# One Strassen pair in the first FFN of blocks 3 to 6, and queries of batches 4 to 7 scaled at their cast

## The chip, the cores and the metric

The kernel runs on 1 core of a Trainium2 chip. The metric is the device time in microseconds (us). It is the span of the trace, from the first to the last instruction, and about 2.2 us more outside of it. The engines are TensorE (PE in the profile; PEld is its weight load), VectorE (DVE), ScalarE (ACT), GpSimd (POOL), and SyncE (SP), which issues the transfers. All runs that are compared here are fast runs with a granted TensorE clock of 0.99 to 1.00. In the profile's lines, L810 is line 810 of that run's kernel. The same statement has another number in each of the two kernels: settle's addition is L810 before and L828 after the change, and scan's addition and multiplication are L522 and L526 before, L533 and L537 after.

## The reference

A retention layer (attention with a decay mask in place of the softmax) feeds a feed-forward network (FFN) with a GELU:

```python
# q, k, v: (8, 8, 576, 64) float32: batch, heads, sequence, head width
scores = (q @ k.transpose(0, 1, 3, 2)) / sqrt(64)
gamma  = 1.0 - 2.0 ** (-5.0 - arange(8))                # one per head
Dmat   = where(i >= j, gamma_h ** (i - j), 0.0)
attn   = (scores * Dmat) @ v
x = attn.transpose(0, 2, 1, 3).reshape(4608, 512)
h = x @ w_in                                            # (4608, 512) @ (512, 2048)
g = 0.5 * h * (1 + tanh(sqrt(2 / pi) * (h + 0.044715 * h**3)))
out = g @ w_out                                         # (4608, 2048) @ (2048, 512)
```

## The kernel before

The work is cut into nine blocks of 512 tokens: Block(b) holds the first 512 tokens of batch b, and Block(None) the last 64 of all eight batches (the "tails"). They run in the order 0, 1, ..., 6, None, 7. Attention runs in chunks, one batch ahead of the FFN: `score_mm` (TensorE) and `mask_sc` (VectorE), `state_mm` (TensorE), `scan` (VectorE) and `put` (a cast of the running state), then `values` and `inter_mm` (TensorE) and `evac` (VectorE).

The first FFN of a block is sixteen columns `up`, each four matmuls of 512 columns and a gelu. The second FFN is one level of Strassen in seven products, my, mz, mw, mv, mu, my2, mz2. The `mix_*` helpers prepare its inputs and `settle` adds its products up. In the last two blocks, four pairs of first-FFN columns are computed by one Strassen level too: `pair_a`, `pair_q`, `pair_b`, `pair_s`, `pair_g`. A pair needs sums and differences of the weights (`forms_w`, ten quarter-tiles for each pair) and of the inputs (`forms_x`, five for each block).

```python
def bank(name, dt=F32):               # all matmul outputs share eight PSUM banks
    return ps.tile([128, 512 if dt == F32 else 1024], dt, tag="bank", name=name)

def score_mm(b, s, hh):
    st = [bank("st") for _ in range(2)]
    ...                               # 16 small matmuls

def scan(b, n, hhs=(0, 1)):           # reads the banks of state_mm
    ...
    if n > 0:
        nc.vector.tensor_tensor(out=t, in0=uc, in1=a["w", n - 1][:, qs], op=ALU.add)        # vs
    nc.vector.tensor_tensor(out=a["w", n][:, qs], in0=uc, in1=gt..., op=ALU.mult)           # ws

def evac(b, s, c):
    nc.vector.tensor_tensor(out=xb[b]..., in0=att[b]["x", s][c]..., in1=gx, op=ALU.mult)

class Block:
    def up(self, f):
        hp = bank("hp")
        for ct in range(4):
            nc.tensor.matmul(hp, w_in_sb[:, ct, 128 * f : 128 * f + 128], x[:, :, ct, :], ...)
        nc.scalar.activation(out=self.g(f // 2)[:, f % 2], in_=hp, func=AF.Gelu_apprx_tanh)

    def pair_a(self, j):              # 10 matmuls of 256 columns into three banks
        pv, pw, py = bank("pv"), bank("pw"), bank("py")
        ...
    def pair_q(self, j):              # one ScalarE copy, two VectorE operations
        ...
    def pair_b(self, j):              # 4 more matmuls onto py
        ...
    def settle(self, m, u=None):      # reads the bank of product m
        ...
        if m == "my":   nc.scalar.mul(out=q(0, 1), in_=t, mul=-1.0)
        ...
        elif m == "mv":
            tt(q(0, 0), q(1, 1), ALU.subtract)      # tt: nc.vector.tensor_tensor
            tt(q(0, 1), q(0, 1), ALU.add)
        ...
    def down(self, m):
        self.product(m)
        self.settle(m)
```

In the timelines below each engine works through its instructions in program order, and the program order is a schedule by hand. `units` are the pieces of TensorE's FFN work; `plan` says after which unit a side step is emitted.

```python
def run(units, plan):
    for i, f in enumerate(units):
        f()
        for step in plan.get(i, ()):
            step()
...
units += [L(F2.up, f) for f in range(NF)] + [L(F2.down, m) for m in MS]   # units 56 to 71, 72 to 78
plan = add({},
    ...
    (73, L(mask_tail, 3)),
    (76, L(scan, 4, 0)),
    (77, L(scan, 4, 2)),
    (78, L(put, 4, 0, S2)),           # S2: half on ScalarE, half on VectorE
    (76, L(scan, 4, 1)),
    ...
)
run(units, plan)
...
for t in order:                       # blocks 3 to 6, None, 7: the same plan for each of 3 to 6
    ...
    plan = add({},
        (1, L(values_tail, t)),
        (1, L(score_mm, b, 0, 1)),    # b = t + 1
        (1, L(score_mm, b, 0, 0)),
        (1, L(inter_tail, t)),
        ...
```

## Time and profile before

| before | |
|---|---|
| device time, median (lowest to highest) | 297.97 us (297.75 to 298.04) |
| span of the profiled execution | 295.8 us |
| busy share of the span: TensorE, VectorE, ScalarE, GpSimd | 98%, 80%, 55%, 33% |
| granted TensorE clock | full in every slice |

The busy shares are averages over stages with different limits, and the end of a matmul is estimated, so the table says which engine is full but not where the time goes.

### The profile page before, as it was taken

Reading aid. Unit: us, or ns where it says so; the run is one execution under the profiler, and the core shown is the slowest. Engines: PE = TensorE matmul, PEld = TensorE weight load, DVE = VectorE, ACT = ScalarE, POOL = GpSimd, SP = SyncE. Lnnn points to the kernel's source line nnn. Section 1 sums busy time; section 2 is a strip of 40 time slices with the busy share of each in tenths; the row PEclk is TensorE's granted clock in tenths of the full one; section 3 lists DMA queues with packets and bytes.
Section 4 is the critical chain, followed back from the end, with each engine's and each line's share of the span. In section 5 each row is a group of like instructions: output and inputs, shape, how many; then the busy total and the mean of one; then the engine's idle time right before and its main releaser. Section 6 shows DMA issues by size and latency. Waiting matters only on the chain.

```text
span 295.8 us, 8812 instructions
## 1 busy us (share of the span) xinstructions
PE 289.7 (98%) x3689; PEld 207.1 (70%) x3689; DVE 237.2 (80%) x456; ACT 164.1 (55%) x320; POOL 99.0 (33%) x131
## 2 busy tenths in 40 slices
PE   8999999999999999999999999999999999999995
PEld 5657478888885568656875587558755886787684
DVE  4898889989997999888569856899688198876773
ACT  7449889973736681665446544554445317605830
POOL 4662695056160346075037007698000000000000
PEclk9999999999999999999999999999999999999999
DMA  7999999767899979995996999482120002002204
GB/s 224 336 350 313 307 381 316 201 173 189 219 227 228 298 224 162 286 308 110 215 303 193 161 240 264 121 155 9 58 86 2 1 33 112 2 0 73 71 0 144
DMA packets 92663, 52.48 MB, mean 177 GB/s; under 512 B 38352, under 2 KB 86480, under 8 KB 92624
## 3 DMA queue, kind: packets, MB, share of 16 engines
q1 hardware_dynamic: 92288, 51.26, 65.2%
q10 hardware_dynamic: 336, 0.66, 0.8%
q8 instruction: 29, 0.48, 0.7%
q14 instruction: 10, 0.08, 0.1%
HBM read 36.70 MB, written 9.44 MB: 156 GB/s over the span
## 4 chain that ended last, share of the span: by engine, by line
PE 85%; ACT 4%; DVE 3%; POOL 2%; DMA 2%; SPq 1%; issue 1%; DVEq 0%; POOLq 0%
PE hp L641 29%; PE my L783 10%; PE mz L783 9%; PE hp L727 6%; PE mu L783 5%; PE mv L783 5%; PE mw L783 5%; PE xs L553 3%; PE py L671 2%; PE xs L580 2%; DMA ld<-in_v_dram 2%; PE st L438 2%; POOL cv L260 1%; SPq L197 1%; PE pv L671 1%; PE us L506 1%
## 5 line engine op out<-in xcount | busy, mean ns | idle before, releaser
L641 PE MATMUL hp<-x,w_in_sb 128*128 128x512 f16 x400 | 92.4, 379 | 0.4 <-DVE vs L522 0.2
L645 ACT ACTIVATE gT<-hp 128x512 f16<-128x512 f32 x108 | 63.9, 597 | 43.9 <-PE hp L641 43.1
L641 PEld LDWEIGHTS <-w_in_sb 128*128 128x128 f16 x432 | 40.9, 98 | 42.9 <-issue 0.6
L783 PEld LDWEIGHTS <-gT 128*128 128x128 f16 x576 | 55.8, 98 | 8.1 <-ACT gT L714 0.2
L451 DVE TENSOR_TENSOR ret<-st,cm 128x512 f16<-128x512 f32 x64 | 40.0, 681 | 4.5 <-PE st L438 4.5
L260 POOL TENSOR_TENSOR cv<-ld,sc 128x512 f16<-128x512 f32 x28 | 30.8, 1115 | 33.2 <-DMA ld<-in_v_dram 33.2
L247 POOL CAST kq<-ld 128x512 f16<-128x512 f32 x27 | 18.8, 704 | 56.8 <-DMA ld<-in_k_dram 33.5
L247 ACT CAST tbd<-ws 64x256 f16<-64x256 f32 x56 | 22.3, 402 | 22.3 <-DVE ws L526 21.8
L783 PE MATMUL my<-w_out_sb,gT 128*128 128x256 f16 x288 | 34.5, 273 | 0.0
L783 PE MATMUL mz<-w_out_sb,gT 128*128 128x256 f16 x288 | 34.4, 273 | 0.0
L783 PEld LDWEIGHTS <-gsum 128*128 128x128 f16 x288 | 27.9, 98 | 3.4
L756 DVE TENSOR_TENSOR gT<-gT 128x1024 f16<-128x1024 f16 x35 | 28.8, 842 | 0.2
L752 DVE TENSOR_TENSOR gsum<-gT 128x1024 f16<-128x1024 f16 x35 | 27.8, 795 | 1.3 <-ACT gT L733 0.8
L593 DVE TENSOR_TENSOR x<-xs,gx 128x512 f16<-128x512 f32 x32 | 21.7, 684 | 4.0 <-PE xs L580 3.6
L810 DVE TENSOR_TENSOR ost<-ost,mv 128x512 f32<-128x512 f32 x18 | 11.6, 683 | 11.7 <-issue 7.7
L744 DVE TENSOR_TENSOR gdia<-gT 128x512 f16<-128x512 f16 (+1 forms) x32 | 16.3, 508 | 5.0 <-ACT gT L645 2.6
L727 PE MATMUL hp<-x,w_in_sb 128*128 128x256 f16 x160 | 18.8, 273 | 0.0
L247 ACT CAST kq<-ld 128x512 f16<-128x512 f32 x27 | 16.4, 616 | 4.0 <-DMA ld<-in_q_dram 2.8
L783 PE MATMUL mw<-w_out_sb,gdia 128*128 128x256 f16 x144 | 17.2, 273 | 0.0
L783 PE MATMUL mu<-w_out_sb,gsum 128*128 128x256 f16 x144 | 17.2, 273 | 0.0
L783 PE MATMUL mv<-w_out_sb,gsum 128*128 128x256 f16 x144 | 17.2, 273 | 0.0
L727 PEld LDWEIGHTS <-w_in_sb 128*128 128x128 f16 x160 | 15.3, 98 | 2.2 <-issue 0.3
(119 smaller groups left out, 396.2 us busy)
## 6 DMA issues: line engine op xcount, KB each, us to landing
ld<-in_k_dram SPq DMA_DIRECT2D x30, 256.0 KB, 5.1
ld<-in_q_dram SPq DMA_DIRECT2D x30, 256.0 KB, 5.1
ld<-in_v_dram SPq DMA_DIRECT2D x30, 256.0 KB, 5.5
out_dram<-ost SPq DMA_DIRECT2D x14, 512.0 KB, 4.3
loan<-in_moe_w_out_dram SPq DMA_DIRECT2D x12, 256.0 KB, 5.7
loan<-in_moe_w_in_dram SPq DMA_DIRECT2D x8, 256.0 KB, 7.0
ld<-in_moe_w_in_dram SPq DMA_DIRECT2D x8, 256.0 KB, 5.7
ld<-in_moe_w_out_dram SPq DMA_DIRECT2D x4, 256.0 KB, 5.6
```

The lines of the kernel that those rows point to most:

```text
L247: (eng.copy if eng is nc.scalar else eng.tensor_copy)(out=out, in_=in_)
L260: eng.tensor_tensor(out=unperm(att[b]["v"][:, s, hh, :]), in0=perm(t), in1=sc[:, 8 * hh : 8 * hh + 8] .rearrange("p (r h) -> p r h", r=2) ...
L451: nc.vector.tensor_tensor(out=x.rearrange("p (a m) -> p a m", a=2), in0=st[hl].rearrange("p (a m) -> p a m", a=2), in1=cm.rearrange("p r s ...
L593: nc.vector.tensor_tensor(out=xb[b][:, :, 2 * s + c].rearrange("p s q i -> p q s i"), in0=att[b]["x", s][c].rearrange("p (q s i) -> p q s ...
L641: nc.tensor.matmul(hp, w_in_sb[:, ct, 128 * f : 128 * f + 128], x[:, :, ct, :], start=(ct == 0), stop=(ct == 3),)
L645: nc.scalar.activation(out=self.g(f // 2)[:, f % 2], in_=hp, func=AF.Gelu_apprx_tanh)
L727: nc.tensor.matmul(hp[:, 256 * h : 256 * h + 256], w_in_sb[:, ct, 256 * j + 128 * h : 256 * j + 128 * h + 128], xb[self.b][:, :, 2 * u : 2 ...
L744: e.tensor_tensor(out=self.sa[:, j : j + n], in0=g[:, :, 0, 0:256], in1=g[:, :, 1, 256:512], op=ALU.add)
L752: e.tensor_tensor(out=self.sc[:, j : j + n], in0=g[:, :, 0], in1=g[:, :, 1], op=ALU.add)
L756: e.tensor_tensor(out=g.rearrange("p j h c -> p j (h c)")[:, :, 256:768].rearrange("p j (h c) -> p j h c", h=2), in0=g[:, :, :, 0:256], in ...
L783: nc.tensor.matmul(t[u] if isinstance(t, list) else t[:, 256 * u : 256 * u + 256], lhs(j, slice(128 * u, 128 * u + 128)), w_out_sb[:, j, w ...
L810: nc.vector.tensor_tensor(out=out, in0=in0, in1=t, op=op)
```

## The change

The intent is to take columns from TensorE: the same Strassen pair in blocks 3 to 6 that the last two blocks have. Room for its side work on VectorE comes from scaling q at its cast, so that the eviction of attention becomes a plain copy that ScalarE can share. Many entries of the plan are reordered as well, in the front (everything before block 3) and in the repeated plan.

```diff
+    QS = 4
...
+        elif key == "q" and b >= QS:
+            f = sq[:, 8 * hh : 8 * hh + 8].rearrange("p (r h) -> p r h", r=2)
+            eng.tensor_tensor(out=unperm(o), in0=perm(t), in1=f.unsqueeze(3).to_broadcast([128, 2, 4, D]), op=ALU.mult)
...
-    def evac(b, s, c):
+    def evac(b, s, c, eng=None):
+        if b >= QS:
+            copy(eng, ...)
+            return
...
+    RS, keep = [], [0]                       # three of twelve load buffers kept for the input forms
...
-        def forms_x(self, part):
+        def forms_x(self, part, e=nc.vector):
...
+    BK = {t: Block(t) for t in range(3, B)}
+    SPS = (4,)
...                                           # in the plan of the front; dozens of reordered steps are cut
-        (68, L(put, 3, 2, A)),
+        (64, L(put, 3, 2, A)),
...
+        (60, L(reserve)),
+        (60, L(forms_w, 4, "sc", G)),
+        (64, L(forms_w, 4, "sa", G)),
+        (68, L(forms_w, 4, "d0", G)),
+        (72, L(forms_w, 4, "d1", G)),
+        (74, L(BK[3].forms_x, "sub1", V)),
+        (74, L(BK[3].forms_x, "sub0", V)),
+        (74, L(BK[3].forms_x, "add", V)),
+        (74, L(BK[3].forms_x, "sum0", V)),
+        (74, L(BK[3].forms_x, "sum1", V)),
     )
     run(units, plan)
...                                           # in the repeated plan of blocks 3 to 6
+                (11, L(F.pair_b, 4)),
+                (8, L(F.pair_q, 4)),
+                (12, L(F.pair_g, 4)),
+                (11, L(F.pair_s, 4)),
...
+                (5, L(F.mix_d, 0, 2, G)),
...
+                (15, L(F.mix_sa, 6, 2, G)),
...
+                (17, L(F.mix_sc, 6, 2, G)),
+                (19, L(F.mix_d, 6, 2, G)),
...
+                    (19, L(BK[t + 1].forms_x, "sum1", V)),
+                    (16, L(BK[t + 1].forms_x, "sub1", V)),
...                                           # and three more of these
         ups = [L(F.up, f) for f in range(NF)]
+        if t in range(3, B - 1):
+            for j in SPS:
+                ups[2 * j : 2 * j + 2] = [L(F.pair_a, j), L(int)]
```

## The prediction

> **What bounds the kernel now.** I read the chain of work that ended last first, then the same chain in order of time, then the table of stages, then the groups by shape, and last the waits. The page's chain line says which engine sets the end:
>
> ```profile
> PE 85%; ACT 4%; DVE 3%; POOL 2%; DMA 2%; SPq 1%; issue 1%; DVEq 0%; POOLq 0%
> ```
>
> TensorE holds 85% of it, and the chain in order of time (columns: start, length, what) shows that from 125 us on nothing else appears before the last stores. One block of the steady part:
>
> ```profile
> 181.88 1.73 PE hp L641 x8
> 183.79 0.45 PE st L438 x32
> 184.46 4.32 PE hp L641 x20
> 188.78 0.57 PE xs L553 x32
> 189.35 0.45 PE st L438 x32
> 190.12 4.32 PE hp L641 x20
> 194.63 0.45 PE xs L553 x32
> 195.07 0.52 PE us L506 x63
> 195.59 0.55 PE xs L580 x8
> 196.15 3.45 PE hp L641 x16
> 199.60 1.75 PE my L783 x16
> ```
>
> Pieces follow one another without a hole, so a column taken from TensorE here shortens the run by its own length, as long as nothing else becomes late. The lengths also give the real rates: 20 matmuls of 512 columns in 4.32 us are 216 ns each, 16 of 256 columns in 1.75 us are 109 ns each. The groups list 379 and 273 ns for the same two shapes, because successive records overlap, so I price by spacing.
>
> The table of stages (window, its length, then busy time of TensorE, weight loads, VectorE, ScalarE and GpSimd with counts, then clock, DMA share and GB/s), for the stages of blocks 4, 5 and 6 (the third has no more loads), shows how much room the helpers have:
>
> ```profile
> 151.90:181.90 30.00, 30.00 (x401) 20.38 (x400) 23.18 (x41) 15.78 (x30) 11.81 (x16) 1.00 0.98 223
> 181.90:211.80 29.90, 29.90 (x401) 20.34 (x400) 25.69 (x41) 15.89 (x30) 21.14 (x25) 1.00 0.45 93
> 211.80:241.70 29.90, 29.90 (x351) 20.05 (x349) 19.85 (x40) 11.32 (x19) 0.00 (x0) 1.00 0.09 37
> ```
>
> TensorE is full; VectorE has 4 to 10 us free in a block, ScalarE 14, GpSimd 9 to 30. The DMA share of 0.98 falls to 0.09, so loads run ahead and end early. The device time is 297.97 us against a span of 295.8, a constant 2.2 us outside.
>
> **What the Trainium skill says.** "TensorE: Matmul & The Clock Gate", section "Back-to-back issue gap", gives 518 cycles for 512 columns and 262 for 256 at 2.4 GHz, 216 and 109 ns: the trace agrees with both. The same section's 131 ns per 512-column matmul in a real stream is not what this trace has. "Perfetto Trace Analysis", section "Tensor Engine Instruction", says that the end of a matmul record is estimated; that fits records (379 ns) longer than their spacing (216), and is why I ignore "98% busy". "GPSIMD Engine Reference", section "Engine selection", calls two-input elementwise work about twice as slow there as on VectorE; here it is more: the 512-element difference of the gelu output takes 1156 ns on GpSimd and 419 on VectorE in the last stage above. "SBUF — State Buffer", section "Who interferes with whom", says that a VectorE instruction with two SBUF inputs contends with a GpSimd instruction that reads SBUF. The trace agrees: the 1024-element sum on VectorE took 683 ns in the stage where GpSimd did nothing and 1161 ns where GpSimd was busy for 21.14 us.
>
> **The change, part by part.**
>
> 1. The Strassen pair. In each of blocks 3, 4, 5 and 6, two columns of the first FFN are now eight matmuls of 512 columns, 8 x 216 = 1.73 us. The pair takes four into pv, two into pw, four into py and four more into py: 14 of 256 columns, 14 x 109 = 1.53 us. The saving is 0.20 us a block, four blocks 0.81 us. The kernel before has the same pair in its last two blocks, so the price is seen there: three runs of 4, 2 and 4 matmuls take 1.10 us and the later four 0.43 us.
>
> 2. What the pair asks of others. These are the groups by shape (count, then busy time and mean ns of one, then idle time before):
>
> ```profile
> L693 DVE TENSOR_TENSOR q<-pw,q 128x512 f32<-128x512 f32 x8 | 5.5, 692 | 0.3
> L690 DVE TENSOR_TENSOR q<-py,q 128x512 f32<-128x512 f32 x8 | 5.5, 687 | 3.3 <-ACT q L689 3.3
> L708 DVE TENSOR_TENSOR q<-py,q 128x512 f32<-128x512 f32 x8 | 5.5, 684 | 0.5 <-PE py L671 0.5
> L667 DVE TENSOR_TENSOR xf<-x 128x512 f16<-128x512 f16 x5 | 1.8, 418 | 0.0
> L744 POOL TENSOR_TENSOR gdia<-gT 128x512 f16<-128x512 f16 x2 | 2.3, 1156 | 1.5 <-ACT gT L645 1.5
> L260 POOL TENSOR_TENSOR cv<-ld,sc 128x512 f16<-128x512 f32 x28 | 30.8, 1115 | 33.2 <-DMA ld<-in_v_dram 33.2
> L593 DVE TENSOR_TENSOR x<-xs,gx 128x512 f16<-128x512 f32 x32 | 21.7, 684 | 4.0 <-PE xs L580 3.6
> ```
>
> VectorE gains three pair operations (0.69 + 0.69 + 0.68 = 2.06) and five input forms (5 x 0.42 = 2.10). It also takes one v cast and two tail casts from GpSimd (about 1.0 + 2 x 0.41 = 1.8). Scaling q at its cast frees the eviction of batches 4 to 7 from its factor: it becomes a plain copy, and two of four go to ScalarE (2 x 0.68 = 1.37), as does half of the tail's (0.29). Four of the twelve mixes go to GpSimd (two of 0.42 and two of 0.69, 2.2). Net: 2.06 + 2.10 + 1.8 - 1.37 - 0.29 - 2.2 = +2.1, so some 25.3 us of 29.8 in block 4, perhaps 27 with more contention. The stage with 25.69 us held TensorE up nowhere.
>
> GpSimd: the usual casts of a batch are 9.6 us (4 x 1.115 + 5 x 0.704 + 2 x 0.46 + 0.69). It gains four mixes (2 x 1.16, 2.13 and 2.57, the last two from the single instances on GpSimd, 7.0 in all) and multiplications in four q casts for plain ones (4 x 1.115 + 0.704 - 5 x 0.704 = 1.6), and gives up 2.3. That is 16 us of 30. ScalarE: +1.2 for two copies, +0.4 for the tail, +0.58 for pv, and one gelu of 1.06 for two of 0.60: +2, about 18 of 30. The weight forms of the pair come once, some 3 x 0.87 + 1.29 = 3.9 us on GpSimd during block 2, where it waited 12.3 us for one q load. All of this lies beside TensorE.
>
> 3. The reordering before block 3. It removes no TensorE work there; some padding matmuls grow and some shrink. Outside the last stage TensorE lost only about 2 us in start-up and little after, so there is not much to win: I give it -0.15 us, a guess with no row behind it, between -0.5 and +0.3.
>
> Sum: 297.97 - 0.81 - 0.15 = 297.0 us.
>
> **The rivals.**
>
> A. The second half of the pair (pair_b) waits for VectorE, which must have read py first. VectorE works in order, and score masks stand ahead of it. In block 5 before, the four masks ran from 189.84 to 192.3; the pair's first half would stand at about 190.8 to 192.0. The copy and first addition (0.58 + 0.69) could then be done by 194. Two ups (1.73) and the attention products of that unit (0.57 + 0.13 + 0.54 + 0.55) lie between, until about 195.7: some 1.5 us of slack. Against it: a busier VectorE queue. If it fails, up to 1 us a block, so 298 to 301.
>
> B. Three of the twelve load buffers are set aside for the input forms, so nine loads of a batch can run ahead instead of twelve. The last two v loads then go out near 184, when the first casts free buffers, and land some 5.5 us later (the median of the v loads), are cast by 192, and the state product runs at 195.1. The slack of about 3 us stands behind GpSimd's longer queue. If it fails, 1 to 3 us in each of three blocks: 300 to 306. For it: the profile has GpSimd waiting up to 15.8 us for single k loads. Against it: those waits ended long before any product needed them.
>
> C. Mixes on GpSimd come late for the second FFN. After the last gelu (0.6 us behind the last up), the three late ones end 1.8, 3.9 and 6.5 us into the second FFN by the durations above. The sum is read in mv at about 5.9 (5.24 + 0.65) and the difference in my2 at about 9.4: slack of 2 us and more. Cost if wrong: a few tenths a block.
>
> D. The opposite: shorter queues in blocks 3 to 6 and a smoother front win more than the columns, 296.3.
>
> **Range and chances.** The columns are near certain (0.8 us). The rest is small waits: a few tenths lost in A to C would end at 297.5, a good front at 296.4. Full failures of A or B are unlikely, since each has slack in the trace, and the order of all steps was plainly fitted anew. 80% range 296.3 to 297.8. Two per cent are 6 us: no part of the change can win that, only B at its worst could lose it.
>
> **What would show it.** Right: stages of blocks 3 to 6 shorter by 0.2 us each, fourteen pair matmuls in 1.53 us, no wait of TensorE on VectorE or GpSimd, VectorE at 25 to 27 us a block, GpSimd near 16. The first fault to look for is a hole in TensorE just ahead of pair_b (A), ahead of the state product (B), or inside mv or my2 (C). A front (before block 3 begins) that moved by more than 0.5 us either way would make my number wrong with the pair's working intact.

## More of the kernel before

The chain of work that ended last and the table of stages say more; the prediction shows them. One part of the chain in order of time (start us, length us, what) that it does not show matters later:

```profile
117.19 1.29 DVE ost L810 x2
...
118.91 0.43 DVE vs L522
...
119.79 0.60 DVE ost L810
```

From 117.16 to 125.21 the path to the end runs through VectorE (`settle`, `scan`), GELUs and casts on ScalarE, and not through TensorE. These are the 8 us around the border of blocks 2 and 3. TensorE is busy there, but its work is not what later work waits for.

## The result

The changed kernel took 301.44 us (median of four runs, 301.39 to 302.33), against 297.86 us (four runs, 297.71 to 298.04) for the kernel before on the same chip. The ratio is 1.0127, with a 95% interval of 1.0107 to 1.0147. Here and below a ratio is the mean time of one kernel's fast runs over that of the other's of the same rounds, so it is not quite the ratio of the medians quoted. The change is within 2% of the time before, but slower by 3.6 us and outside the predicted range. The spans are 295.8 and 299.4 us.

The page's chain line of the changed kernel already says that something stands beside TensorE now:

```profile
PE 70%; DVE 9%; POOL 8%; ACT 5%; issue 3%; DMA 2%; SPq 2%; DVEq 0%; POOLq 0%; ACTq 0%
```

TensorE's share fell from 85% to 70%, and VectorE's and GpSimd's rose from 3% and 2% to 9% and 8%. (SPq and the other names with a q are the queues of the engines.)

**Where the 3.6 us are.** I cut both spans at the first matmul of the product my in blocks 0, 2, 3 and None, and read the starts from the timeline of TensorE. The last two columns are single distances: from the first score matmul at the border of blocks 2 and 3 to the inter product that follows it, and from the start of product mv to the start of mu in block 6.

| us | to my of block 0 | to my of block 2 | to my of block 3 (holds the border) | to my of block None (holds blocks 4 to 6) | to the end | border | mv to mu, block 6 |
|---|---|---|---|---|---|---|---|
| before | 56.8 | 51.5 | 31.3 | 115.0 | 41.3 | 0.55 | 1.75 |
| changed | 57.0 | 52.6 | 33.4 | 115.1 | 41.3 | 2.82 | 2.22 |

The front lost 1.4 us (my of block 2 starts at 109.61 against 108.25), the stage with the border 2.2 (33.42 against 31.26), the stage with three pairs 0.1, the last none. Together these are the 3.6 us.

**The pair itself pays.** The chain in order of time of the changed kernel, in the steady part (start us, length us):

```profile
164.53 0.44 PE pv L689 x4
164.97 0.22 PE pw L689 x2
165.19 0.44 PE py L689 x4
...
169.11 0.44 PE py L689 x4
```

The fourteen matmuls of a pair take 0.44 + 0.22 + 0.44 + 0.44 = 1.54 us in place of 1.73, and no hole stands before `pair_b`. From my to my in the same chain, block 4 shrank from 29.98 to 29.80 us and block 5 from 29.95 to 29.81.

The stages of blocks 4, 5 and 6 (window, length, busy time with counts of TensorE, weight loads, VectorE, ScalarE and GpSimd, then clock, DMA share and GB/s):

```profile
155.40:185.20 29.80, 29.80 (x408) 20.98 (x406) 27.88 (x45) 16.70 (x32) 16.66 (x13) 1.00 0.73 189
185.20:215.00 29.80, 29.80 (x408) 20.98 (x406) 27.88 (x45) 16.83 (x33) 20.51 (x17) 1.00 0.52 132
215.00:245.20 30.20, 29.90 (x357) 20.60 (x354) 20.30 (x39) 14.07 (x27) 16.89 (x16) 1.00 0.09 37
```

TensorE is still full in the first two. The third is 0.3 us longer than the stage of block 6 before, and TensorE is busy for 0.3 us less than its length.

**The waits.** TensorE's list of waits (line, releaser, then us in total, how often, longest) has new entries:

```profile
PE st L449 <- DVE ost L828: 0.9, 1, 0.9
...
PE st L449 <- DVE vs L533: 0.9, 1, 0.9
...
PE mv L801 <- POOL gsum L770: 0.3, 1, 0.3
```

The first two are one place, the border. This is VectorE's and TensorE's work there in the kernel before, from the timeline (start us, busy us, instruction, count, and in brackets the idle time before it and what ended it, where "issue" is nothing that the profile shows):

```profile
115.50 1.28 DVE L810 TENSOR_TENSOR ost<-ost,mv 128x512 f32<-128x512 f32 x2 [0.18 <-issue]
117.19 1.29 DVE L810 TENSOR_TENSOR ost<-ost,mu 128x512 f32<-128x512 f32 x2 [0.41 <-PE mu L783]
...
122.47 0.68 DVE L810 TENSOR_TENSOR ost<-ost,mz 128x512 f32<-128x512 f32 x1
...
123.13 0.62 PE L438 MATMUL st<-T 64*64 64x128 f16 x32
```

And the same place in the changed kernel:

```profile
117.80 2.25 DVE L685 TENSOR_TENSOR xf<-x 128x512 f16<-128x512 f16 x5
119.97 1.27 DVE L828 TENSOR_TENSOR ost<-ost,mv 128x512 f32<-128x512 f32 x2
...
125.56 0.42 DVE L533 TENSOR_TENSOR vs<-us,ws 128x256 f32<-128x256 f32 x1
...
126.43 0.68 DVE L828 TENSOR_TENSOR ost<-ost,mz 128x512 f32<-128x512 f32 x1
...
124.70 0.46 PE L449 MATMUL st<-T 64*64 64x128 f16 x16
126.04 0.21 PE L449 MATMUL st<-T 64*64 64x128 f16 x1 [0.88 <-DVE vs L533]
127.17 0.41 PE L449 MATMUL st<-T 64*64 64x128 f16 x15 [0.92 <-DVE ost L828]
```

Read it from the top. The five input forms of block 3 stand in VectorE's queue ahead of the settle of mv and take 2.25 us. Before, VectorE had stood idle for 0.18 us ahead of the settle of mv, and for 0.41 us ahead of that of mu, for which it waited for TensorE; now it never waits there. It comes 4.47 us later to the settle of mv (119.97 against 115.50) and 3.96 us later to the settle of mz (126.43 against 122.47), while TensorE comes to its score products only 1.57 us later (124.70 against 123.13). The second half of these products needs two PSUM banks. One is freed by the last scan addition, which ends at 125.98, and the matmul starts at 126.04; the other by the settle of mz, which ends at 127.11, and the matmul starts at 127.17. TensorE stands still for 0.88 + 0.92 us, and the whole border takes 2.82 us in place of 0.55, or 2.27 us more.

The chain in order of time of this same profile does not go through VectorE at the border. It goes back from TensorE's next columns (128.04) to a gelu and a put on ScalarE, and from there to a k load that lands at 126.77. Three load buffers fewer could make loads late, so this is a rival. But ScalarE was busy with that put until 126.96. It had begun it at 126.55, 0.04 us after the scan's last multiplication ended (126.09 + 0.42):

```profile
126.55 0.82 ACT L255 CAST tbd<-ws 64x256 f16<-64x256 f32 x2 [0.58 <-DVE ws L537]
```

So the load held nothing up. In the second profile of the changed kernel (E12), whose border is as long, the chain runs through the forms, the settles and the scan to the same put and gelu (start us, length us):

```profile
113.97 5.36 DVE xf L685 x5
119.33 0.66 DVE ost L828 x2
...
125.37 0.44 DVE ws L537
...
126.67 0.61 ACT gT L663
127.32 5.86 PE hp L659 x20
```

"PSUM — Partial Sum Buffer" of the Trainium skill, section "Specifications (TRN2)", gives eight banks and says that GpSimd reads none of them. So scan and settle cannot leave VectorE and ScalarE, while the forms, which read SBUF, can move. No instruction of this kernel on GpSimd reads a bank, so the traces do not test it; the experiments use it.

**Block 6.** GpSimd's and TensorE's timeline around the wait inside mv, with the same columns:

```profile
232.86 1.28 POOL L762 TENSOR_TENSOR gdia<-gT 128x512 f16<-128x512 f16 x1 [3.31 <-ACT gT L663]
234.10 2.40 POOL L331 TENSOR_TENSOR wf<-w_in_sb 128x512 f16<-128x512 f16 x3
236.46 2.12 POOL L770 TENSOR_TENSOR gsum<-gT 128x1024 f16<-128x1024 f16 x1
...
238.63 1.26 PE L801 MATMUL mv<-w_out_sb,gsum 128*128 128x256 f16 x10 [0.30 <-POOL gsum L770]
```

In block 6 GpSimd also makes the weight forms of the last two blocks' pairs. Its queue is in order: it waits 3.31 us for the last gelu, does one mix, then three weight forms (2.40 us), which nobody needs yet, and only then the sum that mv reads. TensorE waits for that sum; mv takes 2.22 us in place of 1.75.

### The profile page after: what moved, and what is told of

Read it like the earlier page. It is cut to its first block, busy times and chain, and to the rows that moved or that the text cites. A ratio compares the mean times of both kernels' runs of the same rounds, so it can differ in the third digit from the quotient of the medians.

```text
span 299.4 us, 8928 instructions
## 1 busy us (share of the span) xinstructions
PE 290.5 (97%) x3713; PEld 209.7 (70%) x3713; DVE 252.9 (84%) x466; ACT 170.7 (57%) x335; POOL 138.0 (46%) x143
## 4 chain that ended last, share of the span: by engine, by line
PE 70%; DVE 9%; POOL 8%; ACT 5%; issue 3%; DMA 2%; SPq 2%; DVEq 0%; POOLq 0%; ACTq 0%
PE hp L659 22%; PE my L801 7%; PE mz L801 6%; PE hp L745 6%; PE mv L801 4%; PE mu L801 4%; PE py L689 3%; POOL wf L331 3%; PE mw L801 3%; PE st L449 2%; DVE ost L828 2%; DVE ret L462 2%; PE xs L564 2%; DMA ld<-in_k_dram 2%; PE pv L689 2%
## 5 line engine op out<-in xcount | busy, mean ns | idle before, releaser
L659 PE MATMUL hp<-x,w_in_sb 128*128 128x512 f16 x368 | 86.0, 379 | 0.5 <-ACT gT L663 0.2
L663 ACT ACTIVATE gT<-hp 128x512 f16<-128x512 f32 x100 | 58.2, 596 | 35.6 <-PE hp L659 34.7
L659 PEld LDWEIGHTS <-w_in_sb 128*128 128x128 f16 x400 | 38.0, 98 | 38.7 <-issue 0.7
L774 POOL TENSOR_TENSOR gT<-gT 128x1024 f16<-128x1024 f16 x11 | 24.5, 2225 | 51.4 <-PE py L689 36.1
L271 POOL TENSOR_TENSOR cv<-ld,sc 128x512 f16<-128x512 f32 x25 | 27.7, 1126 | 32.0 <-DMA ld<-in_v_dram 17.6
L255 POOL CAST kq<-ld 128x512 f16<-128x512 f32 x13 | 9.2, 713 | 36.3 <-DMA ld<-in_k_dram 16.2
L770 DVE TENSOR_TENSOR gsum<-gT 128x1024 f16<-128x1024 f16 x31 | 24.2, 782 | 0.5 <-ACT gT L663 0.4
L774 DVE TENSOR_TENSOR gT<-gT 128x1024 f16<-128x1024 f16 x25 | 20.2, 824 | 0.5
L685 DVE TENSOR_TENSOR xf<-x 128x512 f16<-128x512 f16 x25 | 18.7, 778 | 0.0
L762 DVE TENSOR_TENSOR gdia<-gT 128x512 f16<-128x512 f16 (+1 forms) x28 | 14.4, 516 | 3.6 <-ACT gT L732 2.2
```

The costliest lines, as they stand in the source:

```text
L255: (eng.copy if eng is nc.scalar else eng.tensor_copy)(out=out, in_=in_)
L271: eng.tensor_tensor(out=unperm(att[b]["v"][:, s, hh, :]), in0=perm(t), in1=sc[:, 8 * hh : 8 * hh + 8] .rearrange("p (r h) -> p r h", r=2) ...
L685: e.tensor_tensor(out=o.rearrange("p c (n i) -> p c n i", n=i0.shape[2]), in0=i0, in1=i1, op=op)
L770: e.tensor_tensor(out=self.sc[:, j : j + n], in0=g[:, :, 0], in1=g[:, :, 1], op=ALU.add)
L774: e.tensor_tensor(out=g.rearrange("p j h c -> p j (h c)")[:, :, 256:768].rearrange("p j (h c) -> p j h c", h=2), in0=g[:, :, :, 0:256], in ...
```

## The experiments

Twelve kernels ran. E1 to E4 ran on one chip, E5 to E7 on a second, E8 to E10 on a third, E11 and E12 on a fourth; each group shares its runs of the kernel before. Single fast runs of one kernel scatter by up to 2.4 us for the kernel before (297.31 to 299.69 on the third chip) and up to 3.8 us for a changed one (E4), so where less than 1 us matters I read the stage table and the trace instead of the medians. The main theory was the border: forms ahead of scan and settle in VectorE's queue. Its rivals were the new order of the front, and the scaling of q at its cast, whose multiplications lengthen the queues ahead of the border.

| us, profiled execution | to my 0 | to my 2 | to my 3 | to my None | to the end | border | mv to settle | mv to mu |
|---|---|---|---|---|---|---|---|---|
| before | 56.8 | 51.5 | 31.3 | 115.0 | 41.3 | 0.55 | 2.01 | 1.75 |
| changed | 57.0 | 52.6 | 33.4 | 115.1 | 41.3 | 2.82 | 4.90 | 2.22 |
| E1 front as before | 58.6 | 51.7 | 33.9 | 115.0 | 41.6 | 2.82 | 4.90 | 2.21 |
| E3 weight forms early | 57.4 | 51.8 | 32.6 | 115.0 | 41.3 | 2.24 | 4.34 | 2.22 |
| E4 no q scaling | 56.4 | 52.0 | 35.1 | 117.3 | 41.4 | 2.81 | 4.91 | 2.54 |
| E5 no pair in block 3 | 56.7 | 52.4 | 31.3 | 115.0 | 41.3 | 0.65 | 2.74 | 2.22 |
| E6 E3 and forms on GpSimd | 57.3 | 51.9 | 32.0 | 115.0 | 41.7 | 1.60 | 2.76 | 2.21 |
| E7 E6 and mixes of block 6 back | 57.0 | 52.6 | 31.5 | 114.5 | 41.9 | 0.56 | 2.23 | 1.75 |
| E8 no pairs | 56.6 | 52.1 | 31.5 | 115.5 | 41.3 | 0.55 | 2.19 | 2.09 |
| E9 E7 and one put back | 56.7 | 52.0 | 32.5 | 114.5 | 41.9 | 0.79 | 2.00 | 1.75 |
| E10 E9 and front as before | 57.7 | 51.9 | 31.6 | 114.5 | 41.6 | 1.15 | 2.16 | 1.75 |
| E11 E10 without the pair in block 3 | 57.1 | 53.0 | 31.2 | 114.5 | 41.3 | 0.55 | 2.01 | 1.75 |
| E12 changed kernel again | 56.7 | 52.4 | 34.7 | 115.0 | 41.3 | 2.84 | 4.94 | 2.21 |

The table of the stages, for all profiles that can be read. "mv to settle" is the distance from the first matmul of mv in block 2 to the start of its settle, so it says how far VectorE is behind TensorE just ahead of the border.

Two cells under "to my 3" are longer than the waits explain: E4 (35.1) and E12 (34.7), against 33.4 for the changed kernel's first profile with the same border. There the granted clock fell to 0.50 right after the border, for about 3.4 us (from 127.2 in E4, from 126.7 in E12). The twenty matmuls of 512 columns that follow took 6.09 and 5.79 us from first start to the next instruction, in place of 4.41. A stage row of E12 (the clock is the third number from the end), its twenty matmuls, and those of the first profile:

```profile
128.00:130.00 2.00, 2.00 (x6) 0.76 (x5) 2.00 (x4) 1.18 (x3) 0.29 (x1) 0.50 0.49 135
...
127.32 5.86 PE L659 MATMUL hp<-x,w_in_sb 128*128 128x512 f16 x20
...
128.04 4.48 PE L659 MATMUL hp<-x,w_in_sb 128*128 128x512 f16 x20 [0.23 <-ACT gT L663]
```

Of the 21 fast runs of kernels with a border of 2.2 us or more (the changed kernel, E1, E3, E4, E12), eight have a clock of 0.993 or 0.994. Of the 41 fast runs of the other variants, three are that low (0.992 to 0.994), and none of the 40 of the kernel before in these experiments is under 0.998. So in some executions the hole may cost 1.3 to 1.6 us on top. That the hole brings the slower clock about was not tested, and for the runs without a profile it is not known where the clock fell.

### E1: the front in the old order

The order of loads, of padding matmuls and of plan steps up to unit 59 is put back to that of the kernel before. The new forms, the scaled q, the reordered steps from unit 60 on and the blocks' plan stay. In this document "old front" means this edit.

```diff
-    load_w_out(14, H)
     load_w_out(7, E3)
+    load_w_out(14, H)
...
-        (52, L(put, 2, 2, A)),
+        (52, L(put, 2, 2, G)),
...        # and every other reordered line up to unit 59
```

> The changed kernel with everything before block 3 (load order, padding counts, order of steps up to the second FFN of block 1 and the first steps of block 2) put back as before; pair, q scaling and all that follows stay. If the reordering costs the 1.58 us by which the changed kernel is late at the start of block 3's first FFN, the time falls to about 299.9 us (301.44 - 1.58). If that lateness comes from other parts (the weight forms and q multiplications on GpSimd slowing VectorE), it stays within 0.4 us of 301.4.

Measured: 302.63 us (before: 298.52), ratio 1.0132 [1.0102, 1.0162]. The changed kernel's excess is fully there, and the border is as long as before the edit, 2.82 us. The order of the front up to there is not the cause. The stage to my of block 2 fell from 52.6 to 51.7 us, while that to my of block 0 was 1.6 us longer in this execution, so this run does not say what the new order costs by itself.

### E2: block 3's input forms on GpSimd

```diff
-        (74, L(BK[3].forms_x, "sub1", V)),
+        (74, L(BK[3].forms_x, "sub1", G)),
...        # likewise the other four
```

> The changed kernel with block 3's five input forms on GpSimd instead of VectorE; nothing else. If VectorE's queue at the border of blocks 2 and 3 is the cause of the 2.4 us hole in TensorE there, the 2.25 us of forms leave it and the hole shrinks to below 0.5 us: about 299.3 us. If the hole comes from the rest of VectorE's lateness (GpSimd contending, q cast on VectorE), the time stays above 300.7 us.

Measured: the three fast runs took 300.27, 299.94 and 301.25 us, ratio 1.0066 [1.0034, 1.0097]. About 1.8 us (0.6%) of the 3.6 are back. That lies between what the theory and the rivals expected. By the ratio, about 299.8 us beside the first 297.86, it is nearer to the theory (299.3) than to the rivals (above 300.7); by the times on this chip it is not. The profiled execution can't be compared: it took 593.25 us, with every matmul at half pace from start to end (sixteen of 512 columns in 7.44 us, where other runs take 3.45). So where the rest of the excess stands in this kernel was not seen; E6 has the same edit and a good profile.

### E3: the weight forms before the border

```diff
-        (60, L(forms_w, 4, "sc", G)),
-        (64, L(forms_w, 4, "sa", G)),
-        (68, L(forms_w, 4, "d0", G)),
-        (72, L(forms_w, 4, "d1", G)),
+        (55, L(forms_w, 4, "sc", G)),
...        # all four at 55
```

> The changed kernel with the pair's four weight forms run some 10 us earlier, in GpSimd's idle time before block 2's casts. If contention between GpSimd's weight forms and VectorE's 1024-element sums (1.56 us for one that takes 0.68 alone, 1.26 for a difference of 0.42) is what makes VectorE late, 1 to 1.7 us come back: about 300.0 us. If the five input forms alone make it late, it stays at 301.0 to 301.5 us.

Measured: 299.96 us (299.08 to 302.16; before 298.52), ratio 1.0059 [1.0014, 1.0104]. The border fell from 2.82 to 2.24 us, and "mv to settle" by as much, from 4.90 to 4.34. The five forms themselves shrank from 2.25 to 1.77 us in this profile, because no weight form ran on GpSimd beside them. So the weight forms are a smaller part of the border, by contention. The larger part stays with the input forms in VectorE's queue. Of this profile's 2.3 us over the kernel before, 1.4 are still in the stage with the border and 0.9 in the front.

### E4: no scaling of q at its cast

```diff
-    QS = 4
+    QS = B
```

> The changed kernel with the scaling of q taken back for all batches: plain q casts on the same engines, evictions again multiply and all stand on VectorE; pair and orders stay. If the q multiplications (a 1.53 us one on VectorE, longer ones on GpSimd) drive the loss at the border of blocks 2 and 3, it falls to about 300.5 us there; but if moving half the evictions to ScalarE is needed to keep VectorE ahead in blocks 4 to 6, holes appear there and the time rises above 301.5 us.

Measured: 303.07 us (301.22 to 305.03), ratio 1.0153 [1.0095, 1.0212]. It is no faster than the changed kernel: its two runs at full clock took 301.22 and 301.98 us, the other two (0.993 and 0.994) are the slower ones. The border is unchanged at 2.81 us, and the stage with blocks 4 to 6 grew from 115.1 to 117.3. The scaling is not the cause; it does what it was meant for, and the pairs would cost more without it.

### E5: no pair, and no forms, in block 3

```diff
-        (74, L(BK[3].forms_x, "sub1", V)),
...        # and the other four
-        if t in range(3, B - 1):
+        if t in range(4, B - 1):
...        # pair_q, pair_b, pair_s and pair_g are left out for t == 3
```

> The changed kernel without the pair in block 3 alone: its two columns are plain again and its five input forms at the border of blocks 2 and 3 are gone; weight forms, q scaling and the pairs of blocks 4 to 6 stay. If those five forms (2.25 us in VectorE's queue) open the hole at the border, its 2.2 us shrink to about 0.3 us, against 0.2 us lost with block 3's pair: 299.5 us, or 1.005 of before. If VectorE's lateness there is mostly GpSimd's doing, at least 1.2 us of the hole stay.

Measured: 300.00 us (before: 298.10), ratio 1.0061 [1.0031, 1.0091]; border 0.65 us. The timeline of VectorE and TensorE at the border, with the columns of above:

```profile
117.11 1.27 DVE L828 TENSOR_TENSOR ost<-ost,mv 128x512 f32<-128x512 f32 x2
...
123.57 0.68 DVE L828 TENSOR_TENSOR ost<-ost,mz 128x512 f32<-128x512 f32 x1
...
124.00 0.71 PE L449 MATMUL st<-T 64*64 64x128 f16 x32
```

Without the five forms the settle of mv follows the tail mask at once, the settle of mz ends before TensorE comes back to the score products, and all 32 of these run without a pause. The stage to my of block 3 is 31.3 us as before, though it gives up that block's pair gain. This shows the forms in VectorE's queue to be the cause of the border's hole. The 0.9 us by which this profile is still longer than that of the kernel before stand in the front (my of block 2 at 109.11 against 108.25).

### E6: E2 and E3 together

> Both moves at once, the weight forms earlier and block 3's five input forms on GpSimd. If the two causes add up (the early weight forms took 0.6 us off the hole at the border and about 0.9 us of smaller holes ahead of it), the hole at the border is under 0.4 us and the time about 298.2 us, 1.001 of before. If GpSimd's input forms come too late for the pair, or slow VectorE's scans, a new hole stands ahead of the pair's third product, and the time stays at 299.5 us or more.

Measured: 299.59 us (before: 298.10), ratio 1.0045 [1.0013, 1.0077]; border 1.60 us. Both expectations, 298.2 us and a border hole below 0.4 us, were missed. VectorE was nearly in time for the settle of mv (2.76), so the queue was mended; but one operation of the scan that follows was stretched (VectorE's timeline, columns as above):

```profile
122.04 1.37 DVE L537 TENSOR_TENSOR ws<-vs,gt 128x256 f32<-128x256 f32 x1
```

The same operation takes 0.42 us elsewhere in this stretch. GpSimd was working on the forms at that moment, and E10, with the forms there too, has 1.16 us for it. So forms on GpSimd no longer stand ahead of the scan, but can still slow it down; the score products then waited 0.81 us for the settle of mz. In E7 the moments fell otherwise and no hole remained.

### E7: E6, and block 6's late mixes back on VectorE

```diff
-                (15, L(F.mix_sa, 6, 2, G)),
+                (15, L(F.mix_sa, 6, 2, V if t == B - 2 else G)),
...        # likewise mix_sc 6 at 17 and mix_d 6 at 19
```

> As the run before, and in block 6 the last three mixes are back on VectorE, so that they no longer stand behind or between the weight forms in GpSimd's queue. If that is what cost the 0.7 us in block 6's second FFN, the hole ahead of mv goes and the time is 0.6 to 0.8 us less: about 297.5 us, 0.998 of before. If that stage is slow for another reason, it stays where the run before was.

Measured: 299.76 us (299.33 to 302.96; before 298.10), ratio 1.0069 [1.0033, 1.0105]. The timed gain that I expected is not seen. The trace does show the point at issue, product mv of block 6:

```profile
235.49 1.91 PE L801 MATMUL mv<-w_out_sb,gsum 128*128 128x256 f16 x16
```

All sixteen matmuls run in one piece, mv to mu takes 1.75 us, and the stage with blocks 4 to 6 fell from 115.1 to 114.5 us. So the hole in mv came from GpSimd's queue, and it cost some 0.5 us. The last stage was 0.6 us longer here, but not by this edit: E6 has 41.7 us without it, E11 41.3 with it, and TensorE's part, from the my of block None to the last mz, takes 35.99 us (255.61 to 291.60) against 35.98 in the changed kernel. The 0.6 us come after it.

### E8: no pairs at all in blocks 3 to 6

```diff
-    SPS = (4,)
+    SPS = ()
...        # no forms_w of pair 4, no forms_x in blocks 3 to 6, no pair_q, pair_b, pair_s, pair_g there
```

> The changed kernel with the pairs of blocks 3 to 6 taken out whole: plain columns, no input forms there, no weight forms for them; q scaling, reserved buffers, mixes on GpSimd and all orders stay. If the pair's side work costs the time (2.2 us hole at the border, 0.6 to 0.9 us of weight forms ahead of it) and TensorE gains 0.8 us by it, this runs at 299.3 us or less, 1.002 to 1.006 of before, and faster than the changed kernel although TensorE has more columns. If the new orders and the scaling are what costs, it stays above 301 us (1.011).

Measured: 299.33 us (before: 298.27), ratio 1.0041 [1.0011, 1.0071]; border 0.55 us, stage with blocks 4 to 6 115.5. TensorE has 0.8 us more to do than in the changed kernel, and the kernel is faster: the intervals of the ratios (1.0011 to 1.0071, and 1.0080 to 1.0142 in E12) don't meet. As scheduled here, the pairs' side work costs more than the pairs save. What remains over the kernel before, some 0.4%, is the rest of the change. Part of it is the hole inside mv of block 6: mv to mu takes 2.09 us here, so that hole does not need the pairs of blocks 3 to 6.

### E9: E7, and one put back in its place

```diff
-        (64, L(put, 3, 2, A)),
+        (68, L(put, 3, 2, A)),
```

> The repair of the run with both moves and the last mixes, and the put of state 2 of block 3 back to four units later, where it no longer runs right behind another put on ScalarE. If that put delays two gelus and so a PSUM bank, the 0.3 us hole at 104 us goes and the time is about 299.3 us (0.3 us under the run with both moves and the last mixes, 1.005 of before); if not, it stays as it was, 1.006 to 1.007.

Measured: 299.62 us (298.85 to 302.52; before 298.27), ratio 1.0064 [1.0025, 1.0104]. The stretch near 104 us, where two puts in a row on ScalarE delay a gelu in the changed kernel, is mended: sixteen matmuls of 512 columns take 3.62 us there in place of 3.91. But this execution had a new wait:

```profile
136.61 0.32 PE L517 MATMUL us<-cv,kq 64*64 64x64 f16 x16 [1.14 <-POOL cv L271]
```

The state product waited 1.14 us for a v cast on GpSimd. It is the kind of wait that rival B of the prediction feared: GpSimd itself had waited 0.58 us for the v load. E8 has a small one at the same place (0.27 us). The changed kernel's own two profiles do not have it.

### E10: E9 with the old front

> The same repair, with the order before block 3 as in the kernel before as well. If the new order costs about 0.5 to 1 us between block 0's second FFN and block 2's, as single profiles suggest, this falls to about 298.0 us or below, 0.997 to 1.001 of before. If the front's order is neutral, it equals the repair with the new order within 0.4 us.

Measured: 298.86 us (298.12 to 301.34; before 298.27), ratio 1.0026 [0.9993, 1.0060]. It is the best of the repairs, and not distinguishable from the kernel before. GpSimd needed 5.78 us for the five forms in this run, 1.16 us each, against 0.45 us each on VectorE in the first profile of the changed kernel. Its border is 1.15 us for the reason given at E6.

### E11: pairs from block 4 on

E10 without block 3's pair and its forms, with the weight forms on GpSimd at unit 74. The border has no new work of VectorE at all.

> The last repair with the old front, with pairs in blocks 4 to 6 only: no input forms at the border of blocks 2 and 3, and the weight forms moved into GpSimd's idle time just after that border's casts. If what is left above the kernel before is the work at that border, the time is 0.6 us (three pairs) under before: about 0.998 of it. If the rest of the change (q scaling, fewer load buffers ahead, the ones moved to GpSimd) costs as much by itself, it stays at 1.002 to 1.004 as the last repair.

Measured: 298.77 us (before: 298.06), ratio 1.0029 [1.0006, 1.0052], where 0.998 was expected. The border is clean (0.55 us) and blocks 4 to 6 take 114.5 us, 0.5 less than before. The excess is in the front: 57.1 + 53.0 = 110.1 us against 108.3 before. Two holes of it are in the trace, near 105 and 108 us, where TensorE waits 0.33 and 0.26 us for a score mask and an eviction on VectorE. No version that I tried beats the kernel before.

### E12: the changed kernel once more

> The changed kernel itself once more, on the same chip as the run beside it, to have a second profile of it. The ratio should be 1.011 to 1.015 again; the hole at the border of blocks 2 and 3 (2.2 us) and the one ahead of mv in block 6 (about 0.5 us) should stand in it unchanged if they come from the order of work. The small holes before block 2's second FFN (0.6 us near 89 us) may differ, as they did between runs with the same front.

Measured: 302.13 us (before: 298.06), ratio 1.0111 [1.0080, 1.0142]; one run of 305.37 us with a clock of 0.986 was slow. The border takes 2.84 us again, mv to mu 2.21. So the two holes belong to the kernel and not to one execution, and E11 is compared with the changed kernel on the same chip. The way to the hole is not always the same. Here GpSimd's mix of the gelu output began 1.6 us later than in the first profile (116.00 against 114.37), VectorE's own mix ran freely (0.69 us instead of 2.49), and the forms met the contention in its place (VectorE's timeline):

```profile
113.89 5.44 DVE L685 TENSOR_TENSOR xf<-x 128x512 f16<-128x512 f16 x5
```

They took 5.44 us, and the settle of mv came 4.94 us after mv began, as in the other profiles that have the forms there and the weight forms in their place (4.90, 4.90, 4.91).

## Why the prediction was wrong

**What held.** Part 1, the columns: the pair's fourteen matmuls take 1.54 us as priced, and a steady block is 0.18 and 0.14 us shorter. The pair operations cost 689, 692 and 687 ns, as priced. Rival A did not happen: no profile that can be read lists a wait before `pair_b`. GpSimd at 16.66 us in block 4 is what part 2 said (20.51 in block 5).

**The step that failed** is the close of part 2, "All of this lies beside TensorE". It was argued from busy sums over whole blocks of the steady part, where 2 us more on VectorE fit. But the first set of input forms, that of block 3, is not in the steady part. It stands at the border of blocks 2 and 3, in VectorE's queue, in the 8 us where the path to the end of the kernel before ran through VectorE and ScalarE. I read that path only "from 125 us on". E5 shows it: without these five instructions the border is 0.65 us. The hole measured 2.27 us, in a stage that lost 2.2 us with its pair gain. None of the rivals A to C named this place. The weight forms were misplaced too: part 2 put them into GpSimd's wait of 12.3 us for a q load, which begins at 115.4 in the kernel before and at 118.8 in the changed one. They ran at 85.2, 104.8, 112.6 and 117.9, all ahead of it, while VectorE was busy; E3 moves them and takes 0.6 us off the border.

**A size was off as well.** The forms were priced at 0.42 us from the last blocks, where GpSimd is idle. The groups by shape of the changed kernel show more (count, busy us, mean ns, idle before), and below them stand one long form of block 4 and the GpSimd mix beside it, from the timeline:

```profile
L685 DVE TENSOR_TENSOR xf<-x 128x512 f16<-128x512 f16 x25 | 18.7, 778 | 0.0
...
L685 DVE TENSOR_TENSOR xf<-xt 128x512 f16<-128x512 f16 x5 | 1.9, 420 | 0.1
...
145.93 2.00 DVE L685 TENSOR_TENSOR xf<-x 128x512 f16<-128x512 f16 x1
...
145.35 2.30 POOL L770 TENSOR_TENSOR gsum<-gT 128x1024 f16<-128x1024 f16 x1
```

The mean of 778 ns is a mixture: the median is 419. In each of blocks 3, 4 and 5, three of the five forms for the next block stay short, and two stand beside GpSimd's mixes and take 1.33 to 2.34 us; each of the four in blocks 3 and 4 ends 0.28 or 0.29 us after the mix does (147.93 against 147.65 in the lines above). The prediction had quoted this contention for another instruction and did not apply it to its own sum. Five forms come to 4.5, 5.5 and 4.5 us, not 2.1, and VectorE came to 27.88 us where 25 to 27 were predicted. In the steady part that was still free.

**Rival C happened, for another reason.** The slack of "2 us and more" was worked out with an otherwise empty GpSimd queue. That is right for blocks 3 to 5. In block 6 the weight forms of the last pairs stand between the mixes, and TensorE waits inside mv. E7 shows it; the cost was about 0.5 us, nearly what the pairs of blocks 4 to 6 gained (3 x 0.2). "A few tenths a block" was right in size, once.

**Part 3** gave the front -0.15 us, a guess by its own words; it lost 1.4, and the prediction had named a front that moves by more than 0.5 us as a sign of being wrong. Found in the trace: a hole of 0.40 us near 89 us, where the tails' values wait for the tail mask on VectorE (0.15 to 0.40 in five profiles of the new front, none in four others, none in any with the old one), and 0.3 us near 104 us, where sixteen matmuls take 3.91 us in place of 3.62 because two puts in a row delay a gelu (gone in E9). The rest was not settled: it varies by execution, and it doesn't follow the order of the front alone, since E11, with the old front, has 1.8 us too.

**Range.** "Only B at its worst could lose it" named the wrong risk; B appeared only in E9 (1.14 us) and, small, in E8 (0.27). The range of 296.3 to 297.8 covered small waits and left no room for one border where the side work is on the path.

## What to carry to other kernels

When work moves to an engine with room on average, place every instruction of it in that engine's queue, and the first and last set one by one: a steady stage says nothing about its borders. Read the chain in order of time where it leaves the bound engine; what stands there must not get anything put in front of it. Price the new instructions from rows where the neighbouring engine is as busy as it will be.

## What the Trainium skill lacked or had wrong

- "TensorE: Matmul & The Clock Gate", section "What's actually happening", has the array at full rate after one busy window of about 3.4 us. One execution of E2 stayed at half pace for all of its 591.5 us with TensorE 99% busy (sixteen matmuls of 512 columns in 7.44 us against 3.45). Its clock is recorded as 1.00, but its page has no line of the clock, which all other runs have. Under "Seeing it yourself" the page knows of a clock stuck at a quarter for 50 us and more; one at half pace for a whole execution it lacks.
- "GPSIMD Engine Reference", section "Engine selection", says about twice as slow for two inputs. Here it was 1.16 us against 0.42 for an input form (2.8 times), and 2.23 us against 0.82 for the 1024-element difference (2.7 times).
- No page says how soon a matmul follows the release of its bank by another engine's in-order queue. Here it was 0.06 us, twice (125.98 to 126.04, 127.11 to 127.17), so VectorE's queue sets TensorE's start to within 0.1 us.
- "SBUF — State Buffer", section "Who interferes with whom", has the contention but no durations for such a pair of instructions. Here a form on VectorE took 420 ns with GpSimd idle and up to 2.34 us beside a mix on GpSimd, ending 0.28 us after it.
